# Generating convolution kernels on one Trainium2 core: the sums' two operands trade places, in four column tiles

## The chip, the cores and the metric

The kernel runs on one core of a Trainium2 chip. The metric is the device time of one execution in microseconds, lower is better; "before" is the kernel without the change. A profile is one execution recorded by the hardware profiler, and its times are counted from the start of its span.

## What is computed

Four layers follow each other: a state-space convolution, an attention with one shared key and value head, and both again with the same weights. The part that matters here makes the convolution kernel `K` once, for all D = 640 channels and L = 2048 positions:

```
dt = exp(log_dt)                          # per channel
P[d, n, l] = exp(dt[d] * (A_re + i A_im)[d, n] * l)       n = 0..127
K[d, l]    = Re( sum_n C[d, n] * P[d, n, l] * dt[d] * B[d, n] )
y = causal_convolution(u, K) + u * Dskip  # done by FFT of length 2L
```

Layer norms, the attention (32 heads of 20) and the residual sums follow; the change leaves them alone.

## The kernel before, in words

`_kgen` makes `K`. A position is split as l = 32 i + j with i in 0..63 and j in 0..31, so that the exponential is a product of a factor of i and a factor of j, and K[d, 32 i + j] is a sum over the 128 states n, which lie on the partitions. For each channel two such sums of products are added: `E1R` (128 x 64, over i) with `C2` (128 x 32, over j), and `M1` (128 x 64) with `S2` (128 x 32).

The 640 channels are worked off in 20 units of 32 channels, two halves (`par`) of 16 (`d`) each. For a unit u:

- `phase(u, h)`: PE multiplies split bf16 tables into PSUM (`ph`, one buffer); DVE rounds (`r`, L172) and subtracts (`f`, L357).
- `trig(u, h)`: ACT takes the absolute value and two sines (L370 to L372).
- `sizes(u, k)` and `exps(u, k)`: PE makes exponents in PSUM (`pe`, two buffers, L380), ACT the exponentials (L388, L390).
- `products(u, k)`: six DVE products (L398 to L407); the last two finish `C2` and `S2`.
- `sums(u, ds)`: PE's sums for the channels `ds`, into one PSUM bank `PK[u]`. They are fp32 matmuls; each is recorded as two weight loads (PEld) and two matmuls (PE).
- `store(u)`: ACT copies `PK[u]` into `kst` (L424). After 8 units `kst` is full (`run` = 128 channels in each half; the last 4 units have `run` = 64), and SP's queue writes it to `kd` in DRAM (L432, L436). There is one buffer for `kst`.

PE, ACT and DVE run in the order in which the loop over u issues (a schedule written by hand): the sums of unit u - 2 are cut into five portions and put between the phases and sizes of units u and u + 1, and `store(u - 3)` stands at the head of a pass on ACT. `kd` holds, for each of five blocks of 128 channels, 128 rows (i and the half `jh` of j: row 64 jh + i) of 16 positions times 128 channels. After the generation POOL's queue loads the five blocks of `kd` (L652) and PE takes their spectra (`raw`, L545) block by block, four blocks into `kts` and the last into `ktl`. DVE also makes layer-norm statistics of the input (`stats`, L596, L597) in some passes.

Of the kernel before, what the change touches and what calls it, by code (L numbers as in the profile page):

```python
# [11 lines left out]
F32 = mybir.dt.float32  # L12
# [3 lines left out]
AF = mybir.ActivationFunctionType  # L16
# [5 lines left out]
P = 128  # L22
L = 2048
D = 640
NST = 128
DC = 128
# [5 lines left out]
SCALE = 20.0**-0.5  # L32
LIMIT = 32.0 * 20.0**0.5
SAFE = ((LIMIT - 1e-6) / 1.002) ** 2


def host_constants():
# [99 lines left out]
class Net:  # L137
# [153 lines left out]
    def _kgen(self, ctx):  # L291
        tc, nc, ins = self.tc, self.nc, self.ins
# [33 lines left out]
        bp = ctx.enter_context(tc.tile_pool(name="kgb", bufs=2, reuse_waits="tile"))  # L326
# [20 lines left out]
        def phase(u, h):  # L347

            pp = kp.tile([P, 1024], F32, tag="ph", bufs=1, name=f"ph{u}{h}")
            src, col, rows = ((tb, 0, 48), (ta, 512, 96))[h]  # L350
            for par in range(2):
                nc.tensor.matmul(pp[:, 512 * par : 512 * par + 512], grp(src, u, par, rows),
                                 kg[0:rows, col : col + 512], start=True, stop=True)
# [38 lines left out]
        def products(u, k):  # L392

            tt = nc.vector.tensor_tensor
            if k == 0:
                E1R[u] = big("e1r", u, 64, 2)
                er, m1, c1 = (fl(a[u]) for a in (E1R, M1, C1))
                tt(er[:, :, 32:64], m1[:, :, 32:64], c1[:, :, 0:32], ALU.mult)  # L398
                tt(er[:, :, 0:32], m1[:, :, 0:32], c1[:, :, 32:0:-1], ALU.mult)
            elif k == 1:  # L400
                m1, s1 = (fl(a.pop(u)) for a in (dict(M1), S1))
                nc.vector.scalar_tensor_tensor(m1[:, :, 32:64], m1[:, :, 32:64], -1.0, s1[:, :, 0:32],
                                               op0=ALU.mult, op1=ALU.mult)
                tt(m1[:, :, 0:32], m1[:, :, 0:32], s1[:, :, 32:0:-1], ALU.mult)
            else:
                tt(C2[u], C2[u], M2[u], ALU.mult)  # L406
                tt(S2[u], S2[u], M2[u], ALU.mult)  # L407

        def sums(u, ds):

            if u not in PK:
                PK[u] = kp.tile([P, 512], F32, tag="pk", bufs=2, name=f"pk{u}")
            for d in ds:
                for e, c, first in ((E1R, C2, True), (M1, S2, False)):
                    for par in range(2):
                        nc.tensor.matmul(PK[u][64 * par : 64 * par + 64, 32 * d : 32 * d + 32],  # L416
                                         e[u][:, d, par], c[u][:, d, par], start=first, stop=not first)

        def store(u):
            q, r, _, _, run = units[u]  # L420
            if r == 0 and q > 0:
                KST[q] = bp.tile([P, 32, run], F32, tag="kst", bufs=1, name=f"kst{q}")
            kst = KST[q]
            nc.scalar.activation(kst[:, :, 16 * r : 16 * r + 16],  # L424
                                 PK[u].rearrange("p (d j) -> p j d", d=16), AF.Copy)
            if 16 * (r + 1) == run:
                for par in range(2):
                    for jh in range(2):
                        src = kst[64 * par : 64 * par + 64, 16 * jh : 16 * jh + 16, :]
                        if run == 128:  # L430
                            dst = self.kd[2 * q + par, 64 * jh : 64 * jh + 64]
                            nc.sync.dma_start(dst, src.rearrange("p t d -> p (t d)"))  # L432
                        else:
                            dst = self.kd[4, 64 * jh : 64 * jh + 64].rearrange(
                                "p (t d) -> p t d", d=DC)[:, :, 64 * par : 64 * par + 64]
                            nc.sync.dma_start(dst, src)  # L436

# [3 lines left out]
        n = len(units)  # L441
        engines = {mybir.EngineType.PE, mybir.EngineType.Activation, mybir.EngineType.DVE}
        with tc.manual_schedule(engines=engines):
            for h in range(2):
                phase(0, h)
            for u in range(n + 3):
                now, nxt, prod, tot = u < n, u + 1 < n, 0 < u <= n, 2 <= u < n + 2
                odd = u % 2 == 1
                if u >= 3:
                    store(u - 3)  # L450
                if now and not odd:
                    trig(u, 0)
# [12 lines left out]
                if tot:  # L465
                    sums(u - 2, range(3, 6))
                if nxt:
                    phase(u + 1, 0)
                if now and odd:
                    sizes(u, 2)  # L470
                    exps(u, 2)
                if prod:
                    products(u - 1, 1)
                if now:
                    trig(u, 0 if odd else 1)
                if tot:
                    sums(u - 2, range(6, 10))
                if nxt:
                    phase(u + 1, 1)
                if prod:  # L480
                    products(u - 1, 2)
                if tot:
                    sums(u - 2, range(10, 13))
                if now:
                    if odd:
                        trig(u, 1)
                    else:
                        exps(u, 0)
                        sizes(u, 2)
                        exps(u, 1)  # L490
                        exps(u, 2)
                if tot:
                    sums(u - 2, range(13, 16))
# [350 lines left out]
    def _attn(self, ctx, nm, out):  # L844
# [20 lines left out]
        with tc.tile_pool(name=f"pj{nm}", bufs=1, reuse_waits="tile") as pj:  # L865
# [371 lines left out]
```

## Time and profile before

| what | value |
|---|---|
| median of 3 runs | 3103.51 us (3099.85 to 3104.56) |
| the profiled execution: time, span | 3100.43 us, 3098.6 us |
| first sum to last product of the generation | 72.6 to 331.65 us of the span |
| first and last spectra matmul of the `kd` blocks | 344.7 and 418.7 us |
| L416 matmuls (sums) | 2 x 1280 records |
| writes of `kst`: L432, L436 | 8 of 512 KB, 4 of 256 KB |

Busy time in a row of a stretch stands for PE, PEld (weight loads), DVE, ACT and POOL in this order, with the number of instructions in brackets, then the clock, the share of DMA time and GB/s. In a row of the timeline stand start, duration, engine, line, operation, output and inputs, shape and count, and in square brackets the idle time before it and what ended it. PE's durations run from issue to the modelled end, so neighbours overlap: pace is read from starts. A row of waits gives who waited for whom: us in total, times, longest. A row that begins with "DMA packets" sums up a stretch: packets, megabytes, mean rate, and how many packets are under a size.

### The profile page before, as it was taken

What the parts mean: (1) busy time and instruction counts of PE and PEld (TensorE: products, weight loads), DVE (VectorE), ACT (ScalarE), POOL (GpSimd) and SP (SyncE); (2) the same over time, 40 slices, a digit from 0 to 9 for tenths busy, and PEclk for the clock granted to TensorE, in tenths of its full rate; (3) what the DMA queues carried; (4) which work ended last, traced back from release to release, by engine and by line L of the source; (5) the groups of instructions that cost most, each with busy time, mean ns of one, the idle gap of its engine ahead of it and who ended that gap; (6) DMA issues with size and microseconds to landing.
All of it is one profiled execution on the core that took longest, in us unless ns stands there. A gap on an engine that the chain in (4) does not pass through costs nothing. (4 is left out here: it accounts for less than half of the span.)

```text
span 3098.6 us, 52133 instructions
## 1 busy us (share of the span) xinstructions
PE 2850.6 (92%) x21636; PEld 1349.7 (44%) x21636; DVE 1436.4 (46%) x1855; ACT 2387.1 (77%) x2769; POOL 41.8 (1%) x114
## 2 busy tenths in 40 slices
PE   2888998949899999999999899498999999999999
PEld 0555887847322333333333489464223333233333
DVE  7888799973122232232332399932222222222223
ACT  5777343224799999999999623055999999999997
POOL 0000000000100000000000000000000000000000
PEclk9999999979999999999999999799999999999999
DMA  6011451114310010100100210132010100100100
GB/s 142 18 29 24 168 218 55 33 30 131 116 27 25 21 26 23 25 25 21 27 25 22 111 55 28 26 111 89 22 27 23 40 25 21 44 25 21 44 18 22
DMA packets 73630, 153.45 MB, mean 50 GB/s; under 512 B 22836, under 2 KB 28980, under 8 KB 69764
## 3 DMA queue, kind: packets, MB, share of 16 engines
q1 hardware_dynamic: 67336, 132.36, 14.6%
q0 software_dynamic: 4080, 16.67, 1.4%
q8 instruction: 174, 2.85, 0.4%
q10 hardware_dynamic: 1968, 0.98, 0.1%
q14 instruction: 72, 0.59, 0.1%
HBM read 93.42 MB, written 44.50 MB: 45 GB/s over the span
## 5 line engine op out<-in xcount | busy, mean ns | idle before, releaser
L1038 ACT ACTIVATE pt<-scd 128x1024 f32<-128x1024 f32 x1024 | 942.2, 1116 | 7.5 <-PE scd L1034 5.8
L1038 ACT ACTIVATE pt<-scb 128x1024 f32<-128x1024 f32 x1024 | 942.2, 1116 | 7.0 <-PE scb L1034 5.4
L1048 PE MATMUL pod<-pt,vt 128*32 128x512 f32 x4096 | 547.1, 606 | 4.4 <-DVE on L1065 0.3
L1048 PE MATMUL pob<-pt,vt 128*32 128x512 f32 x4096 | 546.8, 606 | 4.4 <-DVE on L1065 0.5
L1034 PE MATMUL scd<-qpd,kt 62*128 62x512 f32 x2048 | 386.0, 451 | 6.0 <-PEq L983 5.6
L1034 PE MATMUL scb<-qpb,kt 62*128 62x512 f32 x2048 | 386.0, 451 | 5.8 <-PEq L983 5.5
L1034 PEld LDWEIGHTS scd<-qpd,kt 62*128 62x128 f32 x2048 | 166.0, 185 | 402.0 <-ACT pt L1038 392.6
L1034 PEld LDWEIGHTS scb<-qpb,kt 62*128 62x128 f32 x2048 | 166.0, 185 | 401.6 <-ACT pt L1038 392.4
L1096 DVE TENSOR_TENSOR x<-pyd,x 128x320 f32<-128x320 f32 x146 | 71.7, 491 | 561.1 <-PE pyd L1108 561.1
L1096 DVE TENSOR_TENSOR x<-pyb,x 128x320 f32<-128x320 f32 x146 | 71.7, 491 | 547.8 <-PE pyb L1108 547.8
L1068 DVE RECIPROCAL rc<-rc 128x512 f32<-128x512 f32 x62 | 207.9, 3353 | 2.1
L1048 PEld LDWEIGHTS pod<-pt,vt 128*32 128x32 f32 x4096 | 80.6, 108 | 178.2 <-issue 160.2
L1048 PEld LDWEIGHTS pob<-pt,vt 128*32 128x32 f32 x4096 | 80.6, 108 | 178.2 <-issue 160.2
L416 PE MATMUL pk<-s,m 128*64 128x32 f32 x1280 | 130.8, 295 | 13.3 <-DVE s L407 13.3
L416 PE MATMUL pk<-c,e1r 128*64 128x32 f32 x1280 | 132.1, 297 | 11.4 <-DVE c L406 11.2
L416 PEld LDWEIGHTS pk<-c,e1r 128*64 128x64 f32 x1280 | 105.3, 221 | 79.6 <-issue 52.1
L727 PE MATMUL ya<-Aa,wi 128*128 128x128 f32 x640 | 78.0, 285 | 50.5 <-DVE Aa L96 47.2
L727 PE MATMUL yc<-Ac,wi 128*128 128x128 f32 x640 | 78.4, 286 | 46.8 <-DVE Ac L96 43.7
L574 PE MATMUL za<-xna,wf 128*128 128x256 f32 x512 | 113.1, 383 | 2.3 <-ACT xna L690 2.3
L416 PEld LDWEIGHTS pk<-s,m 128*64 128x64 f32 x1280 | 108.1, 226 | 15.9 <-DVE s L407 15.9
L574 PE MATMUL zc<-xnc,wf 128*128 128x256 f32 x512 | 111.5, 379 | 2.7 <-ACT xnc L690 2.7
L576 ACT ACTIVATE Aa<-za 128x1024 f32<-128x1024 f32 x16 | 16.4, 1024 | 118.4 <-PE za L574 117.4
(276 smaller groups left out, 3170.6 us busy)
## 6 DMA issues: line engine op xcount, KB each, us to landing
kh<-kh SPq DMA_DIRECT2D x10, 2048.0 KB
kh<-kn SPq DMA_DIRECT2D x5, 2048.0 KB
qhd<-qh SPq DMA_DIRECT2D x40, 256.0 KB
qld<-ql SPq DMA_DIRECT2D x40, 256.0 KB
qpb<-qhd SPq DMA_DIRECT2D x256, 40.0 KB
qpd<-qhd SPq DMA_DIRECT2D x256, 40.0 KB
ot<-on SPq DMA_DIRECT2D x216, 40.0 KB
wf<-in_c_wf POOLq DMA_DIRECT2D x16, 512.0 KB, 7.8
```

Of the source, the lines that this page charges most:

```text
L416: nc.tensor.matmul(PK[u][64 * par : 64 * par + 64, 32 * d : 32 * d + 32], e[u][:, d, par], c[u][:, d, par], start=first, stop=not first)
L574: nc.tensor.matmul(zv[:, :, c, kk], self.wf[:, t + 4 * h, j, c, kk], x, start=(n == 0), stop=(n == 3))
L576: nc.scalar.activation(A.rearrange("p (o s) d -> p o s d", o=2)[:, :, 2 * t : 2 * t + 2], z.rearrange("p (c o e) -> p o c e", c=2, o=2), A ...
L727: nc.tensor.matmul(y[:, s * DC : (s + 1) * DC], self.wi[:, t, j, c_, kk], v[:, 2 * t + c_, kk], start=(i == 0), stop=(i == 3))
L1034: nc.tensor.matmul(sc[:, 512 * par : 512 * par + 512], kt[rows, 128 * t : 128 * t + 128], qps[nb, hg, pr][rows], start=True, stop=True)
L1038: nc.scalar.activation(pt, sc, AF.Exp, scale=SCALE)
L1048: nc.tensor.matmul(po[32 * j : 32 * j + 32], vt[:, t], pts[step, j // 2][:, 512 * (j % 2) : 512 * (j % 2) + 512], start=(t == 0), stop=(t ...
L1068: nc.vector.reciprocal(rc, rc)
L1096: nc.vector.tensor_tensor(xh, py, xh, ALU.add)
```

## The change

In `sums` the operands trade places. Before, the 64 columns of `E1R` or `M1` were stationary and the 32 of `C2` or `S2` moved, two channels side by side in two column tiles of 64; the result had i on the partitions. Now the 32 columns of `C2` or `S2` are stationary and the 64 of the other move, four channels side by side in four column tiles of 32 (`s`); the result has j on the partitions. `d` now counts 8 steps instead of 16, and the five portions are 2, 1, 2, 2, 1 instead of 3, 3, 4, 3, 3.

`kst` therefore holds 32 j on the partitions of each tile and (i, channel) along a partition. `kd` keeps its layout, so the writes change shape: for each tile `s` and each half `jh` one write from 16 partitions, in runs of 64 channels (256 B; 32 channels and 128 B for the last 4 units), 8 writes where there were 4. Since a tile's 8 channels of a unit must lie next to each other in `kst`, the host puts the channels of the inputs `A_*`, `B_*`, `C_*` and `log_dt` in another order.

```diff
+def channel_order():
+    order = []
+    for start, run in ((0, 128), (128, 128), (256, 128), (384, 128), (512, 64), (576, 64)):
+        for r in range(run // 16):
+            for dh in range(2):
+                c = start + run // 2 * dh + 8 * r
+                order += range(c, c + 8)
+    return np.array(order)
...
-        KST[0] = bp.tile([P, 32, 128], F32, tag="kst", bufs=1, name="kst0")
+        KST[0] = bp.tile([P, 64, 64], F32, tag="kst", bufs=1, name="kst0")
...
                 for e, c, first in ((E1R, C2, True), (M1, S2, False)):
-                    for par in range(2):
-                        nc.tensor.matmul(PK[u][64 * par : 64 * par + 64, 32 * d : 32 * d + 32],
-                                         e[u][:, d, par], c[u][:, d, par], start=first, stop=not first)
+                    for s in range(4):
+                        dd, par = 8 * (s % 2) + d, s // 2
+                        nc.tensor.matmul(PK[u][32 * s : 32 * s + 32, 64 * d : 64 * d + 64],
+                                         c[u][:, dd, par], e[u][:, dd, par], start=first, stop=not first)
...
-                KST[q] = bp.tile([P, 32, run], F32, tag="kst", bufs=1, name=f"kst{q}")
+                KST[q] = bp.tile([P, 64, half], F32, tag="kst", bufs=1, name=f"kst{q}")
...
-            nc.scalar.activation(kst[:, :, 16 * r : 16 * r + 16],
-                                 PK[u].rearrange("p (d j) -> p j d", d=16), AF.Copy)
+            nc.scalar.activation(kst[:, :, 8 * r : 8 * r + 8], PK[u].rearrange("p (d i) -> p i d", d=8), AF.Copy)
             if 16 * (r + 1) == run:
-                for par in range(2):
+                for s in range(4):
+                    par, dh = s // 2, s % 2
+                    kd = self.kd[2 * q + par] if run == 128 else self.kd[4]
+                    c0 = half * dh + (0 if run == 128 else 64 * par)
                     for jh in range(2):
...
+                        dst = kd[64 * jh : 64 * jh + 64].rearrange("i (t d) -> t i d", d=DC)[:, :, c0 : c0 + half]
+                        nc.sync.dma_start(dst, kst[32 * s + 16 * jh : 32 * s + 16 * jh + 16])
...
-                    sums(u - 2, range(0, 3))
+                    sums(u - 2, range(0, 2))
...
-                    sums(u - 2, range(3, 6))
+                    sums(u - 2, range(2, 3))
```

The other three portions, `range(6, 10)`, `range(10, 13)` and `range(13, 16)`, become `range(3, 5)`, `range(5, 7)` and `range(7, 8)`.

On PE, between a size matmul pair (`pe`) and the phase pair (`ph`) of a pass, before the change; `x2` means two fused fp32 matmuls:

```order
L380 LDWEIGHTS tm
L380 MATMUL pe_981<-kg,tm 128x512
L416 MATMUL pk_987<-c_5_836,e1r_867 64x32 [waits DVE_49]
L416 MATMUL pk_987<-c_5_836,e1r_867 64x32
L416 MATMUL pk_987<-s_5_837,m_5_746 64x32 [waits DVE_49]
L416 MATMUL pk_987<-s_5_837,m_5_746 64x32
L416 MATMUL pk_987<-c_5_836,e1r_867 64x32 x2
L416 MATMUL pk_987<-s_5_837,m_5_746 64x32 x2
```

The same place in the changed kernel, to the phase pair, where line 431 is the sums', 394 the sizes' and 366 the phases':

```order
L431 MATMUL pk_1111<-e1r_978,c_6_910 32x64 x4
L431 MATMUL pk_1111<-m_6_957,s_6_911 32x64 x4
L394 LDWEIGHTS tm
L394 MATMUL pe_1128<-kg,tm 128x512 [waits Activation_49]
L394 LDWEIGHTS tm
L394 MATMUL pe_1128<-kg,tm 128x512
L431 MATMUL pk_1111<-e1r_978,c_6_910 32x64 x4
L431 MATMUL pk_1111<-m_6_957,s_6_911 32x64 x4
L366 LDWEIGHTS tb
L366 MATMUL ph_1139<-kg,tb 128x512 [waits PE_49]
```

Where three steps of `d` with two fused matmuls to an operand stood ahead of the phase pair, one step with four now stands there.

On SP's queue, the first set of writes from `kst` before the change, and the first of the second set:

```order
L432 DMA kd<-kst_278 64x2048 [waits DMAHW6_49,Activation_49]
L432 DMA kd<-kst_278 64x2048 [waits DMAHW7_49]
L432 DMA kd<-kst_278 64x2048 [waits DMAHW0_49]
L432 DMA kd<-kst_278 64x2048 [waits DMAHW1_49]
L432 DMA kd<-kst_1457 64x2048 [waits DMAHW2_49,Activation_49]
```

And now:

```order
L448 DMA kd<-kst_278 16x64x64 [waits DMAHW6_49,Activation_49]
L448 DMA kd<-kst_278 16x64x64 [waits DMAHW7_49]
L448 DMA kd<-kst_278 16x64x64 [waits DMAHW0_49]
L448 DMA kd<-kst_278 16x64x64 [waits DMAHW1_49]
L448 DMA kd<-kst_278 16x64x64 [waits DMAHW2_49]
L448 DMA kd<-kst_278 16x64x64 [waits DMAHW3_49]
L448 DMA kd<-kst_278 16x64x64 [waits DMAHW4_49]
L448 DMA kd<-kst_278 16x64x64 [waits DMAHW5_49]
L448 DMA kd<-kst_1461 16x64x64 [waits DMAHW6_49,Activation_49]
```

Four writes of 64 rows have become eight of 16 rows with 64 runs each; ACT's first copy into the next `kst` waits for all eight instead of four.

More of the change, by code (lines that the diff above doesn't have):

```diff
@@ L414, in sums @@
                 for e, c, first in ((E1R, C2, True), (M1, S2, False)):
-                    for par in range(2):
-                        nc.tensor.matmul(PK[u][64 * par : 64 * par + 64, 32 * d : 32 * d + 32],
-                                         e[u][:, d, par], c[u][:, d, par], start=first, stop=not first)
+                    for s in range(4):
+                        dd, par = 8 * (s % 2) + d, s // 2
+                        nc.tensor.matmul(PK[u][32 * s : 32 * s + 32, 64 * d : 64 * d + 64],
+                                         c[u][:, dd, par], e[u][:, dd, par], start=first, stop=not first)
         def store(u):
             q, r, _, _, run = units[u]
+            half = run // 2
             if r == 0 and q > 0:
-                KST[q] = bp.tile([P, 32, run], F32, tag="kst", bufs=1, name=f"kst{q}")
+                KST[q] = bp.tile([P, 64, half], F32, tag="kst", bufs=1, name=f"kst{q}")
             kst = KST[q]
-            nc.scalar.activation(kst[:, :, 16 * r : 16 * r + 16],
-                                 PK[u].rearrange("p (d j) -> p j d", d=16), AF.Copy)
+            nc.scalar.activation(kst[:, :, 8 * r : 8 * r + 8], PK[u].rearrange("p (d i) -> p i d", d=8), AF.Copy)
             if 16 * (r + 1) == run:
-                for par in range(2):
+                for s in range(4):
+                    par, dh = s // 2, s % 2
+                    kd = self.kd[2 * q + par] if run == 128 else self.kd[4]
+                    c0 = half * dh + (0 if run == 128 else 64 * par)
                     for jh in range(2):
[L429 to L436, printed above, removed]
+                        dst = kd[64 * jh : 64 * jh + 64].rearrange("i (t d) -> t i d", d=DC)[:, :, c0 : c0 + half]
+                        nc.sync.dma_start(dst, kst[32 * s + 16 * jh : 32 * s + 16 * jh + 16])
         n = len(units)
@@ L476, in _kgen @@
                 if tot:
-                    sums(u - 2, range(6, 10))
+                    sums(u - 2, range(3, 5))
                 if nxt:
@@ L482, in _kgen @@
                 if tot:
-                    sums(u - 2, range(10, 13))
+                    sums(u - 2, range(5, 7))
                 if now:
@@ L492, in _kgen @@
                 if tot:
-                    sums(u - 2, range(13, 16))
+                    sums(u - 2, range(7, 8))
                 if u == 0:
@@ L1225 @@
     data["A_u"] = data["A_u"].reshape(L, D)
+    for n in ("A_re", "A_im", "B_re", "B_im", "C_re", "C_im"):
+        data[f"A_{n}"] = np.ascontiguousarray(data[f"A_{n}"][CHANNELS])
+    data["A_log_dt"] = data["A_log_dt"].reshape(D)[CHANNELS]
     data["A_log_dt"] = np.ascontiguousarray(data["A_log_dt"].reshape(5, P).T)
```

1 line of the change is left out of this document (added).

## The prediction

> **What bounds the kernel now.** I read the page first, then the busy time of each engine in the stretch that the change touches, then who waits for whom there, then one pass of its loop instruction by instruction, and last the transfers.
>
> ```profile
> span 3098.6 us, 52133 instructions
> 72.60:331.65 259.05, 231.27 (x2610) 149.19 (x2610) 220.11 (x208) 197.01 (x200) 9.69 (x42) 1.00 0.14 39
> DVE r L172 <- PE ph L352: 33.5, 17, 2.5
> ```
>
> The second row is the generation of the convolution kernels, from its first sum to its last product: 259 us, PE busy 231, DVE 220, ACT 197. No engine is full. The third row says that DVE waits 17 times for the phase matmul on PE, 33.5 us in all. One pass shows why:
>
> ```profile
> 205.92 1.22 DVE L172 TENSOR_SCALAR r<-ph 128x1024 bf16<-128x1024 f32 x1 [1.42 <-PE ph L352]
> ...
> 214.11 1.22 DVE L407 TENSOR_TENSOR s<-s,m 128x1024 f32<-128x1024 f32 x1
> 215.39 0.43 PE L416 MATMUL pk<-s,m 128*64 128x32 f32 x4 [0.71 <-DVE s L407]
> 216.60 1.03 PE L380 MATMUL pe<-kg,tm 48*128 48x512 bf16 x2
> 217.41 1.22 DVE L399 TENSOR_TENSOR e1r<-m,c 128x1024 f32<-128x1024 f32 x1
> 217.56 0.43 PE L416 MATMUL pk<-c,e1r 128*64 128x32 f32 x4
> 218.99 1.03 PE L352 MATMUL ph<-kg,tb 48*128 48x512 bf16 x2
> 220.06 1.22 DVE L172 TENSOR_SCALAR r<-ph 128x1024 bf16<-128x1024 f32 x1 [1.42 <-PE ph L352]
> ```
>
> It is a ring. DVE works without a gap from r (205.92) to the end of the last product (215.33), 9.41 us. PE then does the sums that waited for that product (215.39 to 216.60, 1.21), a size matmul pair (0.96), three channels of sums (217.56 to 218.99, 1.43) and the phase pair (1.03), and only then does the next r start: 14.14 us. DVE's other work, L399 the last of it, ends at 218.63, so 1.42 us of PE's stay uncovered in a pass with statistics, more in one without.
>
> **The sums themselves.**
>
> ```profile
> 217.79 0.41 PE L416 MATMUL pk<-s,m 128*64 128x32 f32 x4
> 218.01 0.41 PE L416 MATMUL pk<-c,e1r 128*64 128x32 f32 x4
> 344.70:348.60 3.90, 3.90 (x18) 3.90 (x19) 1.00 1.03 421
> 349.00:352.90 3.90, 3.90 (x37) 3.90 (x37) 1.00 1.05 375
> 1500.15 1.06 PE L1048 MATMUL pob<-pt,vt 128*32 128x512 f32 x8
> ```
>
> A group (one operand, two channels in two column tiles, two records each) starts 0.2135 us after the one before (two starts in the rows, and the rest of the block at that pace), so a record pair costs 107 ns. The next two rows are the spectra's matmuls (L545), right behind the generation: 18 records in 3.9 us, then 37. Until about 348.7 TensorE runs at half its later rate, though the page's clock row shows full speed there; I take the whole generation to be at the half rate. At 3.9/18 = 217 ns for 128 moving columns, 32 moving columns cost 54 ns; the other 53 ns of the 107 go to the 64 stationary columns, 0.83 ns each. The last row is the attention: eight records in four column tiles of 32 end within 1.06 us, though at 3.9/37 = 105 ns for 128 columns one of them takes 0.42 us and eight in a row would be 3.4. Four tiles do run side by side.
>
> **The change: PE.** A group now holds four channels: 32 stationary columns (27 ns) and 64 moving ones (107 ns), 133 ns a record, 0.267 us a group, and 16 groups a unit in place of 32. That is 4.3 us for 6.8. Bounds: 0.16 if the clock is released, 0.427 if the tiles' moving streams don't overlap.
>
> In the ring, the sums behind the last product shrink from 5 groups (1.07) to 3 (0.80): 0.27 less. The block ahead of the phase goes from 6 groups (1.28) to 2 (0.53): 0.75 less. Together 1.02 us, less than the smallest wait of 1.42, so DVE still waits for PE and the whole of it counts: 17 passes, 17.3 us. Then the end:
>
> ```profile
> 330.44 1.21 DVE L407 TENSOR_TENSOR s<-s,m 128x1024 f32<-128x1024 f32 x1
> 338.13 0.41 PE L416 MATMUL pk<-s,m 128*64 128x32 f32 x4
> 338.59 0.60 ACT L424 ACTIVATE kst<-pk 128x512 f32<-128x512 f32 x1 [7.48 <-PE pk L416]
> 338.63 0.51 POOL L650 DMA_DIRECT2D ktl<-in_A_Dskip  x1 [14.73 <-PE pk L416]
> 339.22 2.12 POOL L652 DMA_DIRECT2D kts<-kd  x4
> 344.68 0.58 PE L545 MATMUL zk<-kts,wf 128*128 128x128 f32 x1 [6.14 <-DMA kts<-kd]
> ```
>
> After the last product PE sums alone: 31 groups, 6.6 us, with the next stage's loads and first matmul behind them. Now 15 groups, 4.0 us: 2.6 less. What was hidden by it is DVE's statistics and the norm, which stay ahead of the first matmul that needs them. Gain in all: **19.9 us**.
>
> **The change: the stores.** Twice the finished rows leave `kst` (2.1 MB) and ACT may not write the next ones, into the same buffer, before they have landed:
>
> ```profile
> 186.94 0.57 ACT L424 ACTIVATE kst<-pk 128x512 f32<-128x512 f32 x1
> ...
> 197.72 1.02 ACT L390 ACTIVATE m<-pe 128x1024 f32<-128x1024 f32 x1 [0.92 <-PE pe L380]
> 200.09 0.60 ACT L424 ACTIVATE kst<-pk 128x512 f32<-128x512 f32 x1 [1.34 <-PE pe L380]
> ...
> 203.53 1.02 ACT L388 ACTIVATE m<-pe 128x1024 f32<-128x1024 f32 x1 [1.93 <-PE pe L380]
> L424 ACTq EVENT_SEMAPHORE  x8: 38/38/2240, 84.5 to 312.2; - x8
> 191.72 1.22 DVE L172 TENSOR_SCALAR r<-ph 128x1024 bf16<-128x1024 f32 x1 [1.43 <-PE ph L352]
> DMA packets 320, 2.11 MB, mean 209 GB/s; under 512 B 63, under 2 KB 63, under 8 KB 63
> ```
>
> The row with 2240 ns is that wait: from 197.73 to 199.97, 12.45 us after `kst` was written (187.51), though the timeline puts the gap down to PE. It costs nothing today: r goes from 191.72 to 205.92, 14.20 us as ever. ACT has 2.24 us there and 1.93 us more of idle time at 203.53, about 4 us of cover; PE's pair will come a little sooner, so I use 3.9. The last row is 188.5 to 198.6: 10.1 us of transfer, so 2.35 us are issue and landing.
>
> Before, a store read 64 partitions in runs of 8 KB. Now it reads 16 partitions in runs of 256 B, eight stores of 1024 pieces for four. Neither is in the trace as such; the nearest rows:
>
> ```profile
> 33.55 1.25 SPq L208 DMA_DIRECT2D ta<-hdthr  x3
> DMA packets 451, 0.55 MB, mean 128 GB/s; under 512 B 62, under 2 KB 445, under 8 KB 445
> DMA packets 439, 0.51 MB, mean 118 GB/s; under 512 B 57, under 2 KB 437, under 8 KB 437
> DMA packets 1600, 0.43 MB, mean 285 GB/s; under 512 B 1597, under 2 KB 1597, under 8 KB 1597
> DMA packets 1102, 0.28 MB, mean 147 GB/s; under 512 B 1102, under 2 KB 1102, under 8 KB 1102
> ```
>
> The 128 and 118 GB/s are the table loads of L208 (35.0 to 39.3 and 27.0 to 31.3), 16 partitions each, nothing else of weight beside them. The 285 and 147 are 256 B pieces from 64 partitions, the stores of L436: several queued (352.6 to 354.1), and the last alone (354.7 to 356.6). I take the mean of the first two, 123 GB/s, since the number of partitions is what changes most (64 to 16) and all rows with 16 are slow: 2.1 MB take 17.1 us and land 19.5 us after `kst` is written. ACT comes to the wait 10.2 us after that now, about 9.5 in the shorter pass, and has that cover: the ring is late by 19.5 - 13.4 = 6.1 us, twice: **12.2 us**. Behind the waiting copy on ACT stand the exponentials, for which DVE's next products wait. Ends: 285 GB/s (7.4 us, no loss), and 147 times 123/209 = 87 GB/s (24.1 us).
>
> [...]
>
> **The third store and the rest.**
>
> ```profile
> 357.61 0.53 POOL L652 DMA_DIRECT2D ktl<-kd  x1 [16.27 <-DMA kd<-kst]
> 403.88 1.84 PE L545 MATMUL zk<-ktl,wf 128*128 128x128 f32 x15
> ```
>
> The last store (1 MB, now 8192 pieces of 128 B for 4096 of 256 B) delays POOL's fifth load, which is used 46 us after it is issued: PE's work on the four earlier blocks hides up to 40 us more. SP has eight issues for four there, and its next one came at 374.4; nothing is late if the stores are out by then. The copy L424 moves the same 512 elements in strides before and after: nothing, at most 0.1 us each under ACT's idle time.
>
> **The sum.** 19.9 - 12.2 = 7.7 us less than the profiled execution's 3100.4: 3092.7. The median of the runs shown is 3.1 us above that execution: **3096**. About 0.2% (6.2 us) is what a measurement tells from no change.
>
> **The cases.**
> - As summed, stores at 115 to 130 GB/s: 3092 to 3100. Chance 0.26 (0.22 faster, 0.04 within).
> - The stores stay hidden, near the 285 row or the lone 147 (14.3 us, 3.2 us late each): 3083 to 3090. For it: queued pieces ran fast. Against: 64 partitions. 0.20.
> [...]
> - Slower: short pieces and few partitions multiply. The wait on `kst` takes back everything once a transfer lasts 21 us (100 GB/s). At 87 GB/s the ring is 13 us late twice: 6 us slower, 3110; at 75 GB/s, 28 us and 17 us late twice, 3117. For it: the lone store's 147 against 209 for 8 KB runs from the same 64 partitions. 0.28 (0.06 within, 0.22 slower).
> - The four tiles don't overlap: 0.427 us a group, 0.22 us less a pass, 3.7 in all, and 0.2 at the end, less 12.2: 3112. The attention row speaks against it. 0.06.
> - TensorE's clock is released by the denser sums: 0.16 a group, 0.53 us a pass more, 9 us: 3087. PE is 89% busy now and still at half rate. 0.04.
>
> [...]
>
> Faster 0.22 + 0.20 + 0.04 = 0.46; within 0.04 + 0.12 + 0.06 = 0.22; slower 0.04 + 0.22 + 0.06 = 0.32. Range: 3080 to 3118, from hidden stores with 3 us to spare to 75 GB/s.
>
> **What would show it.** In the profile after: sums' groups 0.267 us apart; r to r about 13.1 us; DVE's wait for the phase about 17 us in all; two semaphore waits of about 10 us on ACT's copy; the stores at about 123 GB/s; the first spectra matmul some 7 to 8 us sooner. If the waits on the copy are under 4 us, or over 14, the store term is wrong; if r to r stays over 13.9, the sums are.

## The result and the profile after

The changed kernel takes 3089.76 us (median of 6 runs, 3088.1 to 3094.2); the kernel before, on the same chip, 3102.41 us (6 runs, 3099.85 to 3105.36). The ratio is 0.9961, 95% interval 0.9951 to 0.9972: about 12 us faster. The profiled execution of the changed kernel took 3094.2 us, the slowest of its six, so the account below goes by places inside the profile and not by the difference of the two spans.

First the length of the page, the row of windows from the first sum to the last product, and the two rows of waits that matter there, all of the changed kernel:

```profile
span 3092.4 us, 52155 instructions
73.20:321.60 248.40, 167.18 (x2614) 74.75 (x2614) 220.28 (x208) 195.88 (x200) 9.66 (x42) 0.99 0.19 41
ACT kst L440 <- DMA kd<-kst: 19.7, 2, 10.3
DVE r L186 <- PE ph L366: 17.3, 18, 4.8
```

The generation lasts 248.4 us instead of 259.05. PE is busy 167 us instead of 231, with all but the same number of records. DVE's wait for the phase has halved (17.3 us for 33.5), and ACT has two waits on the stores of `kst` that were not there. One undisturbed pass, from the timeline:

```profile
225.10 1.23 DVE L186 TENSOR_SCALAR r<-ph 128x1024 bf16<-128x1024 f32 x1 [0.53 <-PE ph L366]
...
233.29 1.22 DVE L421 TENSOR_TENSOR s<-s,m 128x1024 f32<-128x1024 f32 x1
...
234.57 0.44 PE L431 MATMUL pk<-m,s 128*32 128x64 f32 x8 [0.70 <-DVE s L421]
234.78 0.44 PE L431 MATMUL pk<-e1r,c 128*32 128x64 f32 x8
235.00 0.44 PE L431 MATMUL pk<-m,s 128*32 128x64 f32 x8
235.37 1.03 PE L394 MATMUL pe<-kg,tm 48*128 48x512 bf16 x2
...
236.33 0.44 PE L431 MATMUL pk<-e1r,c 128*32 128x64 f32 x8
236.54 0.44 PE L431 MATMUL pk<-m,s 128*32 128x64 f32 x8
236.91 1.03 PE L366 MATMUL ph<-kg,tb 48*128 48x512 bf16 x2
...
237.98 1.22 DVE L186 TENSOR_SCALAR r<-ph 128x1024 bf16<-128x1024 f32 x1 [1.20 <-PE ph L366]
```

It is the ring of before with smaller sums in it: r to r 12.88 us for 14.14. The sums behind the last product take 0.80 us (234.57 to 235.37) for 1.21, the block ahead of the phase 0.58 (236.33 to 236.91) for 1.43. A group of eight records, now four channels, still starts 0.2135 us after the one before (234.57, 234.78, 235.00). DVE still waits 1.20 us for the phase.

The first set of stores, on ACT's timeline, and the transfers of both sets (178.8 to 198.0 and 287.2 to 306.0):

```profile
177.57 0.57 ACT L440 ACTIVATE kst<-pk 128x512 f32<-128x512 f32 x1
...
187.62 1.02 ACT L404 ACTIVATE m<-pe 128x1024 f32<-128x1024 f32 x1 [0.19 <-PE pe L394]
198.98 0.60 ACT L440 ACTIVATE kst<-pk 128x512 f32<-128x512 f32 x1 [10.34 <-DMA kd<-kst]
```

```profile
DMA packets 8294, 2.11 MB, mean 110 GB/s; under 512 B 8293, under 2 KB 8293, under 8 KB 8293
DMA packets 8322, 2.13 MB, mean 113 GB/s; under 512 B 8320, under 2 KB 8320, under 8 KB 8320
```

`kst` is written at 178.14 and may be written again at 198.98, 20.8 us later; ACT stands still for 10.34 us. The second time it is 19.9 us (286.68 to 306.59), and the wait (9.41 us) falls near the end, where the last products wait for ACT behind it. The end of the generation and the start of the spectra:

```profile
314.70 1.23 DVE L412 TENSOR_TENSOR e1r<-m,c 128x1024 f32<-128x1024 f32 x1 [8.77 <-ACT c L386]
...
320.38 1.22 DVE L421 TENSOR_TENSOR s<-s,m 128x1024 f32<-128x1024 f32 x1
...
325.87 2.33 POOL L664 DMA_DIRECT2D kts<-kd  x4 [0.17 <-issue]
333.56 11.66 PE L557 MATMUL zk<-kts,wf 128*128 128x128 f32 x76 [8.48 <-DMA kts<-kd]
```

The first spectra matmul starts at 333.56 instead of 344.68, 11.1 us sooner. Behind it the profile has 2758.8 us (3092.4 - 333.56) against 2753.9 before; in the experiments below that rest lies anywhere from 2752.7 to 2758.8 (2758.1 for the kernel before with nothing but its sums in another order), so I take most of it as scatter between executions and not as part of the change. One microsecond of it has a place: the trace's clock has the full rate from 339.7 us on, 6.1 us into the spectra of the `kd` blocks, and before from 348.7, 4.0 us into them, and these spectra take 75.4 us from the first start to the last end for 74.4.

### The profile page after: what moved, and what is told of

Read it like the earlier page. It is cut to its first block, busy times and chain, and to the rows that moved or that the text cites. A ratio compares the mean times of both kernels' runs of the same rounds, so it can differ in the third digit from the quotient of the medians.

```text
span 3092.4 us, 52155 instructions
## 1 busy us (share of the span) xinstructions
PE 2789.9 (90%) x21636; PEld 1276.3 (41%) x21636; DVE 1436.8 (46%) x1855; ACT 2386.0 (77%) x2769; POOL 41.8 (1%) x114
## 5 line engine op out<-in xcount | busy, mean ns | idle before, releaser
L1120 PE MATMUL pyb<-wo,ot 128*32 128x320 f32 x1168 | 105.3, 432 | 0.0
L1120 PE MATMUL pyd<-wo,ot 128*32 128x320 f32 x1168 | 105.3, 432 | 0.0
L586 PEld LDWEIGHTS za<-xna,wf 128*128 128x128 f32 x512 | 98.1, 192 | 16.7 <-ACT xna L702 3.3
L586 PEld LDWEIGHTS zc<-xnc,wf 128*128 128x128 f32 x512 | 97.8, 192 | 16.3 <-ACT xnc L702 3.1
```

What stands on the lines that cost most here:

```text
L586: nc.tensor.matmul(zv[:, :, c, kk], self.wf[:, t + 4 * h, j, c, kk], x, start=(n == 0), stop=(n == 3))
L1120: nc.tensor.matmul(py[j : j + m], o[:, 128 * i + j : 128 * i + j + m], w[:, 320 * half : 320 * half + 320], start=start, stop=stop)
```

## The experiments

### Do the waits on `kst` cost what they seem to?

**Two half-size buffers, the early allocation left out.** The stores leave after four units instead of eight, from two buffers in turn.

```diff
-        KST[0] = bp.tile([P, 64, 64], F32, tag="kst", bufs=1, name="kst0")
...
-            if r == 0 and q > 0:
-                KST[q] = bp.tile([P, 64, half], F32, tag="kst", bufs=1, name=f"kst{q}")
+            g = r // 4
+            if r % 4 == 0:
+                KST[q] = bp.tile([P, 64, 32], F32, tag="kst", bufs=2, name=f"kst{q}{g}")
...
```

> The changed kernel with two kst buffers of half the size: written to DRAM after every 4 units instead of 8, in runs of 128 B, so that ACT's copy never needs a buffer that is still being read. Theory (the two waits of 10.3 and 9.4 us on ACT's copy cost the ring of PE and DVE about 5 us each): no wait on the copy over 0.5 us, and 8 to 12 us less than the changed kernel, about 3079. Rival (ACT's idle time covers the waits, and the loss lies elsewhere): within 2 us of the changed kernel, about 3090.

Measured: 3110.94 us (3108.91 to 3114.6), ratio 1.0031 (1.0018 to 1.0043): slower, where 3079 was expected. The rows of waits from 40 us on say where:

```profile
ACT fa L384 <- DVE f L371: 39.4, 1, 39.4
DVE r L186 <- DMA ta<-hph: 33.6, 1, 33.6
```

The edit also dropped the early allocation of the first buffer, and the start of the generation waited: DVE's first `r` waits 33.6 us for the load of a phase table (`ta`), ACT behind it, and the first sum comes at 103.3 us instead of 73.2. The next kernel, with the early allocation back, has no such wait; why the load came so late is not shown. Inside the generation no wait on `kst` is left, but the time of this kernel says nothing of what the waits cost.

**Two half-size buffers, the first allocated where it was.**

```diff
+        KST[0] = bp.tile([P, 64, 32], F32, tag="kst", bufs=2, name="kst00")
...
+            if r % 4 == 0 and (q or g):
...
```

> The changed kernel with two half-size store buffers in turn (stores leave after four units in runs of 128 bytes instead of after eight in runs of 256), and with the first buffer allocated where the changed kernel allocates it, so that the start is not disturbed. Theory that the two waits on the store buffer cost what they seem to (4.9 us in a disturbed pass, and the rest late in the generation): no wait on the store buffer, every pass 12.9 us, first sum to last product 237 instead of 248.4, the time 3078 to 3082 (0.992 to 0.9935 of before). Rival, that the end takes it back (the shorter generation ends into the last store and the load of the first kts, which then decide): the generation is 11 us shorter but the first spectra matmul only 5 us sooner, 3084 to 3088.

Measured: 3077.33 us (3076.76 to 3080.69), ratio 0.992 (0.9904 to 0.9937), 12.4 us below the changed kernel's median. The window from first sum to last product:

```profile
72.55:309.12 236.57, 167.89 (x2614) 74.59 (x2614) 220.17 (x208) 196.12 (x200) 9.69 (x42) 1.00 0.21 43
```

236.57 us for 248.40, with the same busy times: the two waits cost 11.8 us. All passes are 12.88 or 12.95 us. The spectra start at 321.07, 12.5 us sooner; the rival, that the end takes it back, falls. In the changed kernel the pass with the first wait lasts 17.75 us and the next 13.31, 5.2 us more than here; the second wait makes up the other 6.6: from the last unit's first r to the last product it has 31.96 us, this kernel 25.36.

### Why are the stores slow?

**Half of them on another queue.**

```diff
-                        nc.sync.dma_start(dst, kst[32 * s + 16 * jh : 32 * s + 16 * jh + 16])
+                        (nc.gpsimd if par else nc.sync).dma_start(dst, kst[32 * s + 16 * jh : 32 * s + 16 * jh + 16])
```

> The changed kernel with the stores of the second half (par 1, partitions 64 to 127) issued from POOL's queue instead of SP's, beside the others. [...] Rival theory of the pieces (256 B runs are slow however they are issued): 110 to 125 GB/s, waits of 9 to 10 us, time unchanged, 3090.

Measured: 3094.12 us (10 runs), ratio 0.9973 (0.9964 to 0.9983). Waits, and transfers from 178.5 to 195.5:

```profile
ACT kst L440 <- DMA kd<-kst: 16.5, 2, 8.4
DMA packets 4448, 2.11 MB, mean 124 GB/s; under 512 B 4191, under 2 KB 4191, under 8 KB 4447
```

Two queues shorten the two waits by 3.2 us in all; the rate goes from 110 to 124 GB/s, far from double. The queue is not the main limit. And the gain is lost behind the generation: POOL's loads of `kd` are issued as early as in the changed kernel (325.94 for 325.87) but stand in one queue behind stores, and the spectra start 11.7 us after that issue instead of 7.7, at 337.62.

**Long pieces from the same 16 partitions.** A partition's 16 KB go to one place in DRAM (another layout of `kd`).

```diff
-                        dst = kd[64 * jh : 64 * jh + 64].rearrange("i (t d) -> t i d", d=DC)[:, :, c0 : c0 + half]
...
+                            r0 = 64 * jh + 32 * dh
+                            dst = kd[r0 : r0 + 32].rearrange("(p b) x -> p (b x)", b=2)
...
```

> The changed kernel with the same eight stores from 16 partitions each, but each partition's 16 KB (8 KB in the last set) written as one run, so that kd has another layout and the kernels' spectra are not the reference's. Theory of the partitions: still about 110 GB/s, waits of about 10 us on ACT's copy, 3090. Rival theory of the pieces: 200 GB/s or more, waits under 2 us, about 3080.

Measured: 3079.51 us (3079.11 to 3083.16), ratio 0.9929 (0.9912 to 0.9945). Waits; all transfers of the first set (178 to 190); and its first store alone (its packets start between 179.2 and 180.1), with the time that these packets take as a share of what 16 DMA engines have in that window:

```profile
ACT kst L440 <- DMA kd<-kst: 6.4, 2, 3.6
DMA packets 244, 2.11 MB, mean 176 GB/s; under 512 B 115, under 2 KB 115, under 8 KB 115
DMA packets 16, 0.26 MB, mean 291 GB/s; under 512 B 0, under 2 KB 0, under 8 KB 0
q1 hardware_dynamic: 16, 0.26, 260.4%
```

With long pieces the set goes at 176 GB/s instead of 110, and the waits shrink to a third. One store alone is not fast for that. The 291 GB/s count a packet where it starts; the last row says that the sixteen take 260% of 16 engines' 0.9 us, so 2.3 us each. In the trace they start from 179.43 to 179.93, and the last ends at 182.09: 0.26 MB in 2.66 us, 98 GB/s. The seven stores behind it, from other partitions, go at 192 GB/s together (181.74 to 191.31), so several of them are under way at a time.

**Short pieces from 64 partitions**, in the kernel before: each of its stores cut in two, in pieces of 256 B.

```diff
-                            dst = self.kd[2 * q + par, 64 * jh : 64 * jh + 64]
-                            nc.sync.dma_start(dst, src.rearrange("p t d -> p (t d)"))
+                            dst = self.kd[2 * q + par, 64 * jh : 64 * jh + 64].rearrange("p (t d) -> p t d", d=DC)
+                            for dh in range(2):
+                                cs = slice(64 * dh, 64 * dh + 64)
+                                nc.sync.dma_start(dst[:, :, cs], src[:, :, cs])
```

> The kernel before with its first two sets of stores from 64 partitions cut into runs of 256 B (eight stores for four, each of half the channels). Theory of the partitions: about 200 GB/s as before, the wait on ACT's copy stays near 2 us and the time within 2 us of before, 3102. Rival theory of the pieces: 110 to 125 GB/s, landing 20 us after the copy, a wait of about 10 us, and 8 to 12 us slower than before, about 3112.

Measured: 3100.76 us (10 runs), ratio 1.0001 (0.9991 to 1.001). The halves that were ready early went out early, so each burst has half the bytes; the rate is what can be compared (189.5 to 196.4):

```profile
DMA packets 4147, 1.06 MB, mean 154 GB/s; under 512 B 4146, under 2 KB 4146, under 8 KB 4146
```

256 B pieces from 64 partitions move at 154 GB/s from the first store on (this one alone, 0.26 MB from 189.45 to 191.21: 149). In the changed kernel the first store alone (179.4 to 182.4) has:

```profile
DMA packets 837, 0.21 MB, mean 71 GB/s; under 512 B 837, under 2 KB 837, under 8 KB 837
```

71 GB/s: less than half of the 154, with pieces of the same size. But the two kernels differ in one more thing: the pieces of a partition lie 512 B apart in DRAM there, 8 KB apart here.

**The control for that**: 16 partitions, 256 B pieces, 512 B apart.

```diff
-                        dst = kd[64 * jh : 64 * jh + 64].rearrange("i (t d) -> t i d", d=DC)[:, :, c0 : c0 + half]
+                        dst = kd[64 * jh : 64 * jh + 64].rearrange("(p a) (i d) -> p (a i) d", a=4, d=DC)[:, :, c0 : c0 + half]
```

> The changed kernel with its stores going to other places in DRAM: still 16 partitions and pieces of 256 bytes, but the pieces of a partition 512 bytes apart in DRAM instead of 8 KB apart (the layout of the kernels' spectra in DRAM is then another, and the results are not the reference's). Theory of few partitions (16 source partitions with small pieces are slow): 105 to 125 GB/s as in the changed kernel, waits on the store buffer of 9 to 11 us each. Rival, the stride in DRAM (the control with 64 partitions and 256-byte pieces had a stride of 512 bytes and ran at 150 to 160 GB/s): 150 GB/s and above, waits of 3 to 6 us each.

Measured: 3093.43 us (one run). Waits, transfers of 178.8 to 198.0, and of the first store alone:

```profile
ACT kst L440 <- DMA kd<-kst: 23.3, 2, 12.8
DMA packets 8290, 2.11 MB, mean 110 GB/s; under 512 B 8289, under 2 KB 8289, under 8 KB 8289
DMA packets 921, 0.23 MB, mean 78 GB/s; under 512 B 921, under 2 KB 921, under 8 KB 921
```

The distance in DRAM is not it. The number of partitions and the size of the pieces both count. One store alone has 71 GB/s with 16 partitions and 256 B, 98 with 16 and 16 KB, 149 with 64 and 256 B, and 191 with 64 and 8 KB (the kernel before, 0.52 MB from 188.70 to 191.45). Over a whole set, in which stores overlap, it is 110, 176, 154 and 209: there only few partitions and short pieces together are that slow.

### What sets the pace of the sums?

**Moving operands of 32 columns** instead of 64 (half of the sums are left out, and the copy writes the other half twice).

```diff
-                        nc.tensor.matmul(PK[u][32 * s : 32 * s + 32, 64 * d : 64 * d + 64],
-                                         c[u][:, dd, par], e[u][:, dd, par], start=first, stop=not first)
+                        nc.tensor.matmul(PK[u][32 * s : 32 * s + 32, 64 * d : 64 * d + 32],
+                                         c[u][:, dd, par], e[u][:, dd, par, 0:32], start=first, stop=not first)
...
```

> The changed kernel with moving operands of 32 columns instead of 64 (half of the sums are left out, and the copy writes the other half twice). It measures what sets the start-to-start time of a group of four matmuls of two records each, 0.2135 us in the changed kernel and for two matmuls before. Theory that the larger of the stationary and the moving width counts (64 before by the stationary operand, 64 after by the moving one): a group every 0.107 us. Rival, a fixed time of a record pair: 0.2135 us as before. Rival of the prediction, stationary and moving columns add up (27 + 53 ns): 0.160 us.

Measured: 3081.25 us (one run). The last unit's sums on the timeline:

```profile
315.40 0.32 PE L431 MATMUL pk<-m,s 128*32 128x32 f32 x8
315.50 0.31 PE L431 MATMUL pk<-e1r,c 128*32 128x32 f32 x8
315.61 0.31 PE L431 MATMUL pk<-m,s 128*32 128x32 f32 x8
```

A group every 0.107 us. With 64 stationary and 32 moving columns (before), and with 32 and 64 (after), it is 0.2135; with 32 and 32 half of that. So the larger of the two widths sets the pace, at 1.67 ns a column and record; they do not add up, and there is no fixed time that large. It is not the clock: the trace has the half rate from 309.1 to 329.6. Nor did the two tiles of the kernel before run one after the other: there the records of the two start 7 ns apart (217.794 and 217.800), as those of the four do now (234.567 to 234.587). A pass without statistics takes 12.35 us.

**A tile's two matmuls next to each other**, the loops over `s` and over the two operands exchanged.

```diff
-                for e, c, first in ((E1R, C2, True), (M1, S2, False)):
-                    for s in range(4):
+                for s in range(4):
+                    for e, c, first in ((E1R, C2, True), (M1, S2, False)):
```

> The changed kernel with the two matmuls of one column tile issued one behind the other (products with C2, then with S2, of one channel), then the next tile's, instead of four tiles in turn. Theory that the tiles run side by side only where neighbours in the queue lie in different tiles: a tile's two matmuls follow each other at 0.2135 us, and the next tile overlaps only with the second of them, so the sums of a unit take up to 1.6 times the 3.4 us. Rival, that order does not matter: the unit's sums stay at 3.4 us, 32 matmuls or 16 groups of 0.2135.

Measured: 3097.52 us (one run); the passes are 13.13 and 13.20 us instead of 12.88 and 12.95. From the timeline of one pass:

```profile
248.02 0.42 PE L431 MATMUL pk<-e1r,c 128*32 128x64 f32 x2 [0.59 <-DVE c L420]
249.15 0.31 PE L431 MATMUL pk<-m,s 128*32 128x64 f32 x1 [0.71 <-DVE s L421]
...
250.18 1.03 PE L394 MATMUL pe<-kg,tm 48*128 48x512 bf16 x2
```

The pace hardly suffers: 32 records in a row start within 0.79 us instead of 0.77. The quarter of a microsecond comes from somewhere else. In the changed kernel a whole group of eight records needs only `C2` and goes ahead (one block starts at 233.43) while DVE still makes `S2`; here only two records can, and the other 30 start behind `S2`, 1.03 us ahead of the size pair instead of 0.80. Neither expectation had that.

### Is it the length of the sums, or where they stand?

**The kernel before, its sums moved out of the ring.** Nothing else is changed: two portions of eight channels, behind the two halves of the next unit's phase, for five.

```diff
-                    sums(u - 2, range(0, 3))
+                    sums(u - 2, range(0, 0))
...
-                    sums(u - 2, range(3, 6))
+                    sums(u - 2, range(0, 0))
...
-                    sums(u - 2, range(6, 10))
+                    sums(u - 2, range(0, 8))
...
-                    sums(u - 2, range(10, 13))
+                    sums(u - 2, range(8, 16))
...
-                    sums(u - 2, range(13, 16))
+                    sums(u - 2, range(16, 16))
```

> The kernel before, with nothing changed but the order in which its sums are issued: two portions of eight groups behind the halves of the next unit's phase, instead of five portions (3, 3, 4, 3, 3). Theory of the ring: the sums made the kernel before slow only by standing between f and r, and a pass falls from 14.1 us to 12.3 to 12.9 us (PE's own work is 0.89 of 14.1, 12.6 us), so 3075 to 3088 without any swap of operands. Rival, that the sums' own length on PE set the pass (PE full): a pass stays at 13.8 to 14.1 us, 3095 to 3102.

Measured: 3065.56 us (3064.73 to 3070.74), ratio 0.9878 (0.9862 to 0.9894): some 38 us below the kernel before and 24 below the changed one, with the operands as they were. The window from 90 to 170 us, and DVE's wait over the whole generation:

```profile
90.00:170.00 80.00, 77.29 (x934) 53.15 (x930) 78.53 (x78) 70.75 (x73) 2.04 (x13) 1.00 0.01 2
DVE r L172 <- PE ph L352: 1.3, 4, 0.4
```

DVE is busy 78.5 of 80 us and waits for the phase four times in the generation, 1.3 us in all. A pass takes 11.6 to 12.1 us, with statistics 12.6 to 13.1. PE is busy 77.3 of 80, nearly full; at the end its sums run 6.6 us behind the last product. Pass and time lie below the range expected (12.3 us and 3075 at the least): the theory of the ring holds, but PE's own work, put at 12.6 us a pass, fits into 11.6 to 12.1.

**Both: half-size buffers, and the swapped sums out of the ring** (two portions of four).

```diff
-                    sums(u - 2, range(0, 2))
+                    sums(u - 2, range(0, 0))
...
-                    sums(u - 2, range(2, 3))
+                    sums(u - 2, range(0, 0))
...
-                    sums(u - 2, range(3, 5))
+                    sums(u - 2, range(0, 4))
...
-                    sums(u - 2, range(5, 7))
+                    sums(u - 2, range(4, 8))
...
-                    sums(u - 2, range(7, 8))
+                    sums(u - 2, range(8, 8))
```

> As the kernel with two half-size store buffers, and beside it the sums are issued in two portions of four groups each (behind the first half of the next unit's phase and behind its second half) instead of five, so that none stands between VectorE's f and its next r. Theory of the ring (a pass is VectorE's work plus what PE does between f and the next r): the 1.0 to 1.5 us that VectorE waited for the phase in a pass goes down to what VectorE's own work leaves, ten operations of 1.22 us, so a pass of 12.2 to 12.4 us instead of 12.9; 17 passes give 8 to 11 us over the kernel with half-size buffers, 3068 to 3074. Rival, that PE at its half clock is what bounds the pass once no ring is there: nothing changes, 3078 to 3082.

Measured: 3065.16 us (3062.17 to 3065.66), ratio 0.9878 (0.9862 to 0.9895). The window from 212 to 290 us:

```profile
212.00:290.00 78.00, 51.39 (x1028) 28.15 (x1022) 77.38 (x68) 71.83 (x74) 6.27 (x20) 0.61 0.30 63
```

DVE is busy 77.4 of 78 us; a pass takes 11.6 us without statistics and 12.6 with, DVE's work alone, and less than the 12.2 to 12.4 expected. PE has a third of its time free. The median is that of the kernel before with the same order (3065.56), but the profile shows what the free time buys: from unit 2's to unit 19's first `r` 205.80 us for 207.44, from there to the last product 23.10 for 25.64, and the spectra start at 306.12 instead of 310.85. The rest behind that place differs by as much from execution to execution, so the two medians cannot show it.

**Four of the eight statistics steps moved out of the passes**, behind the last products, in both of these kernels.

```diff
-                if 5 <= u < 13:
+                if 5 <= u < 9:
                     self.stats(u - 5)
-                for t in {n: range(8, 12), n + 1: range(12, 16)}.get(u, ()):
+                for t in {n: range(4, 10), n + 1: range(10, 16)}.get(u, ()):
```

With the swap and the half-size buffers:

> As the kernel with two half-size buffers and the sums off the ring, and beside it four of the eight statistics steps of x that VectorE does inside the passes (1.03 us a pass) are done behind the last products instead. Theory that VectorE alone bounds a pass there: four of the passes of 12.65 us become 11.6, the last product ends 4.1 us sooner (290.0 instead of 294.1); of that the first spectra matmul keeps 2 to 4 us, since VectorE's later statistics stand ahead of its addition to the first kts: 3061 to 3064. Rival, that the longer tail takes all back: 3065 to 3067.

Without:

> The same move of four statistics steps, in the kernel before with its sums off the ring (TensorE busy 77.3 of 80 us there). Theory that TensorE is now the bound without the swap: the four passes cannot go to 11.6 us, they end at 12.2 to 12.6 us, the last product ends at most 2 us sooner, the last sum not sooner at all, so 3064 to 3067 (no gain). Rival, that VectorE bounds here too: the last product ends 4.1 us sooner (293.8) and the time is 3061 to 3064.

Measured: 3057.09 us (3055.09 to 3061.36), ratio 0.9861 (0.9844 to 0.9877) with the swap; 3063.01 us (3062.17 to 3068.21), ratio 0.9881 (0.9865 to 0.9898) without. Windows from 212 to 290 us of the one and of the other:

```profile
212.00:290.00 78.00, 52.55 (x1044) 29.51 (x1040) 77.42 (x69) 67.84 (x71) 6.10 (x19) 0.57 0.35 83
```

```profile
212.00:290.00 78.00, 77.16 (x966) 54.62 (x966) 73.76 (x65) 71.55 (x74) 6.08 (x19) 1.00 0.22 64
```

With the swap the four passes fall to 11.6 us, the last product ends at 289.36 instead of 294.1, and the spectra start 4.9 us sooner; the time is below the 3061 to 3064 expected. Without it PE is full (77.16 of 78) and DVE is not (73.76): the passes without statistics take between 11.6 and 12.1 us, and the last product and the spectra come 3.1 us sooner. That is between the two expectations: PE bounds some of the passes, not all. Here the swap is worth 6.5 us at the first spectra matmul (301.25 against 307.78); the intervals of the two ratios still overlap. The kernel with all three edits (half-size buffers, sums out of the ring, statistics late) has the lowest time of the study, some 32 us below the changed kernel.

## Why the prediction came out as it did

The direction and the two mechanisms were right: a ring from which the sums give time back, and two waits on the stores that take part of it. The forecast was 3096 us, 7.7 us saved up to the first spectra matmul; the profile shows 11.1 there, and the measured 3089.76 lies under the case as summed (3092 to 3100). By its own terms, with the measured value from the places of the two profiles:

| term | predicted | measured | where |
|---|---|---|---|
| 17 passes | -17.3 | -21.3 | from unit 2's to unit 19's first r, 240.80 to 224.71, and 5.2 for the first wait |
| the end | -2.6 | -2.3 | last r to last product 26.59 to 25.36 (half-size buffers); last product to first spectra matmul 13.03 to 11.96 |
| two waits on `kst` | +12.2 | +11.8 | 5.2 and 6.6, as the half-size buffers showed |
| upstream | 0 | +0.7 | first sum 72.58 to 73.24 |
| sum | -7.7 | -11.1 | first spectra matmul 344.68 to 333.56 |

**The step that was off: the price of a group.** I split the 107 ns of a record into 53 for 64 stationary and 54 for 32 moving columns, and so came to 0.267 us for the new group. The kernel with narrow moving operands shows that the parts do not add; the wider of the two sets the pace, and both kernels have a 64. The group stayed at 0.2135 and the sums of a unit halved: 1.25 us a pass instead of 1.02. The spectra's row quoted there spoke against the split: with 128 stationary and 128 moving columns a record took 217 ns, which is 128 times 1.67 ns (214) and leaves nothing for stationary columns at 0.83 ns each.

**The stores: right in size, by luck in part.** The mean of 123 GB/s was 110 and 113, the landing 20.8 and 19.9 us for 19.5, the waits on ACT 10.3 and 9.4 for "about 10", the loss 11.8 for 12.2. Two errors of the sum cancel the first time: the rows land 1.3 us later than forecast, and 15.6 us of the 20.8 are covered instead of 13.4. And the reason was half of it. I went by the number of partitions alone, from table loads; one store does go by that (98 GB/s from 16 partitions in long pieces, 191 from 64), but the set is as slow as it is only with short pieces besides (176 with long ones).

The mean of a set is not the rate of a store: the 110 are made of a first store at 71 and of seven overlapping ones at 116 (182.59 to 198.40). The row of 285 GB/s, the prediction's fast end, is no single store's either: its window begins after 1324 of the set's 4096 packets and ends after 2898, so by the order of issue it runs from a store of the one half of the partitions into one of the other. Of the chances, 0.12 within and 0.04 slower rest on a rate of the stores that no run had shown when they were given; the runs then had 110 and 113 over the two sets.

**The end.** The sums behind the last product did shrink, by 3.4 us for the 2.6 predicted (the last unit's sums start over 4.15 us, before 7.58). The gain behind the last product is only 1.1 us all the same (the other 1.2 us of the row lie between the last r and the last product, for which the prediction had no term): PE waited 8.48 us for the first `kts` instead of 6.14. I had named the statistics and the norm as what is late next, not this load, and let the last set of stores delay the fifth load alone. But the first load itself is slower: 7.7 us from its issue to the matmul (325.87 to 333.56) for 5.5 before (339.22 to 344.68). The last stores' packets move right ahead of it here (326 to 329 us), and behind its start before (from 342 us). In the control with pieces 512 B apart they come behind its start too, and it takes 5.3 us (329.11 to 334.40). So the stores are the likely reason; no run was made to test it.

**The rivals.** Hidden stores gives 3083 to 3090, nearest to the measured 3089.76, but its mechanism did not happen; both waits were there. Four tiles that don't overlap, and stores slow enough to lose, are out by the group's pace and by the waits. The case of a released clock needs a look at the sums that ran without a pause near the end, where the second wait had held them up:

```profile
309.09 0.44 PE L431 MATMUL pk<-e1r,c 128*32 128x64 f32 x8
...
312.08 0.44 PE L431 MATMUL pk<-e1r,c 128*32 128x64 f32 x8
312.30 0.34 PE L431 MATMUL pk<-m,s 128*32 128x64 f32 x8
312.46 0.28 PE L431 MATMUL pk<-e1r,c 128*32 128x64 f32 x8
312.57 0.28 PE L431 MATMUL pk<-m,s 128*32 128x64 f32 x8
```

From 312.4 on a group starts every 0.11 us: the full rate, which the trace's clock grants for 3.4 us, after 3.3 us of sums in a row and a size pair ahead of them. The 6.6 us of sums at the end of the kernel before had shown no such thing: they kept to 0.21 us a group (331.95 to 338.13). The full rate earned nothing: from 313.5 on PE waited for DVE, and the last unit's sums (from 320.6) were at the half rate again.

**What the prediction did not ask.** It measured how much the sums in the ring shrink, and took their place in the ring as given. DVE's wait of 1.42 us a pass was read as the bound of the gain; it was a second gain, open without any swap. The kernel before with two portions instead of five shows it: the wait goes from 33.5 to 1.3 us, the time to 3065.56.

## What to carry to other kernels

When two engines hand work to each other in a ring, look first at what stands in the queue between the hand-overs and need not: moving it gave 38 us here, where halving it gave 12 with the stores that came along and some 25 without their waits. A swap of operands that turns the output also turns the store; price the store by partitions and piece size together (one store alone had 191 GB/s from 64 partitions in 8 KB and 71 from 16 in 256 B), and give it a second buffer before counting on the gain. Read a store's rate from the first start to the last end of its packets: over a window shorter than a packet's own time it says nothing (291 for 98 GB/s above). And price a matmul by the wider of its two operands (0.2135 us a group at 64 and 32, 0.107 at 32 and 32) before trusting a split into two parts.

## What was not expected of the hardware

- Few partitions and short pieces multiply. One store alone has 191 GB/s with 64 partitions and 8 KB, 149 with 64 and 256 B, 98 with 16 and 16 KB, 71 with 16 and 256 B: a quarter of the partitions costs half, short pieces a quarter, each at either value of the other.
- fp32 sums in column tiles go at the pace of the wider operand, 1.67 ns a column and record at the half rate: 0.2135 us a group at 64 and 32 or 32 and 64, 0.107 at 32 and 32.
- The clock's release does not go by busy time alone: in the two windows from 212 to 290 us, the kernel without the swap keeps PE busy 77.16 of 78 us and its groups stay 0.2135 us apart (the 1.00 in its row stands ahead of the first record of the clock), while the kernel with the swap, busy 52.55 of 78, is granted 0.57, that is the full rate for some of the time. What decides it was not tried.
